# More unread identity matmuls in TensorE's waiting times: 31 places in place of 26, in a gated pair of state-space convolutions

## The chip, the cores and the metric

The kernel runs on one core of one Trainium2 chip. The metric is the device time of one execution in microseconds (us). Three runs of the kernel before gave 501.2, 500.29 and 502.1 us; their median is 501.2 us. The engines are called as the profile calls them: PE is TensorE (its matmuls; PEld is its weight loads), DVE is VectorE, ACT is ScalarE, POOL is GpSimd, and SP issues the DMA transfers.

## The reference

An input `x` of 2048 steps by 512 channels goes through two long convolutions, whose filters are sums over 128 complex exponentials in each channel, and a sigmoid of one weighted sum per step mixes the two results. All is float32. Cut to what matters:

```python
def reference(A_u, ..., gate_w):
    def _A_ref(u, A_re, A_im, B_re, B_im, C_re, C_im, log_dt, Dskip):
        dt = jnp.exp(log_dt)[:, None]
        P = jnp.exp((dt * (A_re + 1j * A_im))[:, :, None] * l[None, None, :])
        K = jnp.einsum("dn,dnl,dn->dl", Cc, P, dt * Bc).real
        return causal_convolution(u, K) + u * Dskip      # by FFT of length 2 L
    def _B_ref(u, log_A_real, A_imag, C_real, C_imag, log_dt, D_skip):
        P = jnp.exp((A * dt[:, None])[:, :, None] * pos[None, None, :])
        K = 2.0 * jnp.einsum("dn,dnl->dl", C, P).real
        return causal_convolution(u, K) + u * D_skip
    x = A_u
    g = sigmoid((x * gate_w).sum(-1, keepdims=True))
    return g * _A_ref(x, ...) + (1 - g) * _B_ref(x, ...)
```

(`causal_convolution` stands for the padded FFT, product and inverse FFT that the reference writes out.)

## The kernel before

The 512 channels are taken in four quarters, and each quarter has the two filters: eight filter stages (`NV = 8`). In each stage a filter is built in eight chunks (`chunk`). POOL writes phases `x` and magnitudes `E` (L584, L593, L604, L612), ACT takes sine and cosine of the phases into the PSUM tiles `sd` (L624 to L626), DVE multiplies them with the magnitudes into `QD` and `E` (L632 to L647), and PE sums the products (L663), 64 recorded matmuls a chunk. Every second chunk ACT copies the sums out (`K`, L686), and `put` (L707) takes them through a first Fourier step, two PSUM banks at a time, which ACT or DVE copies out to the tile `F` or `X` (L719). `forward` (L730) is the second Fourier step. For the input itself the same two steps run once for each quarter at the start (`stage1_u`, `stage2_u`; the copies after the second step are L765, written to DRAM at L772). For each filter stage the spectrum is multiplied by that of the input on DVE (`z`, L802 and L805), transformed back on PE (L814, L815), copied out by ACT (`st`, L818) and written to DRAM; `final` (L847) ends a quarter. The gate is a sum by matmul (L876) and a sigmoid.

The order of all this is set before any instruction is written. Each step is put on a list with its engine, a cost and a due time (`Plan.op`), and `Plan.run` plays the list through a model of the engines, the buffers and the PSUM banks, and takes in each engine the ready step with the earliest due time. The instructions are then written in the order found. An engine carries out its instructions in that order, and an instruction that writes into a PSUM bank waits until the last reader of that bank is done.

The table `FILL` (L81) adds matmuls whose result nobody reads. `turn` counts the steps of PE in the order found; where `turn` is a key of `FILL`, a call of `spare` (L143 on) stands in front of that step. It writes the given number of units, each a product of the 128x128 identity with itself, up to four units in one matmul (a matmul of four units is 128x512), into whichever free bank of `ps` or `sd` has been free longest in the model. The spare matmuls cost the model no time, so the table leaves the order of everything else as it is. In the profile they are the matmuls of L310.

A float32 matmul of this kernel appears in the profile as two weight loads and two matmuls: 4,839 matmuls of the program make the 9,678 of PE and 9,678 of PEld.

The lines in `run` that place a spare piece are these:

```python
if e == "T":
    if turn in FILL:
        order.append(self.spare(FILL[turn], min((f, t, i) for t in ("ps", "sd") for f, i in free[t])))
    turn += 1
```

Of the kernel before, what the change touches and what calls it, by code (L numbers as in the profile page):

```python
# [77 lines left out]
FW = -1.82  # L78


FILL = {18: 9, 37: 1, 41: 3, 67: 1, 90: 3, 145: 3, 150: 7, 154: 14, 191: 2, 197: 3, 199: 10, 220: 5, 269: 6, 304: 29, 33: 1, 36: 3, 40: 1, 61: 1, 104: 1, 149: 12, 189: 2, 196: 4, 198: 6, 248: 1, 249: 1, 5: 6}  # L81


def _flat(t):
# [27 lines left out]
class Plan:  # L112
# [44 lines left out]
    def run(self):  # L157
# [15 lines left out]
        while n < len(self.ops):  # L173
            nxt = 1e30
            for e in at:
# [32 lines left out]
# [4 lines that stand above are left out]
# [849 lines left out]
```

## Time and profile before

| | |
|---|---|
| median of three runs | 501.2 us |
| the profiled execution | 501.73 us, of which the span from the first to the last instruction is 499.9 us |
| mean granted clock of PE | 0.98 |
| busy: PE, DVE, ACT, POOL | 89%, 80%, 78%, 79% of the span |
| chain that ended last | PE 33%, ACT 27%, DVE 16%, POOL 11%, issue 10% |
| PE's spare matmuls (L310) | 94 recorded, from 21.1 us to 487.8 us |

The span is the time between the first and the last instruction; the execution's own time is 1.8 us more. Shares of busy time are averages over stages. The chain goes back from the last instruction, at each step to what released it, so that a line of the chain is a time that nothing else covered. "Idle before" names what ended the wait of an engine; "issue" there means that the engine waited for nothing that the profile shows. In the timeline and the chain the first number is the start and the second the duration, in us from the start of the span.

### The profile page before, as it was taken

How to read it: one execution, taken by the hardware profiler on the slowest of the kernel's cores; microseconds unless marked ns; L12 is line 12 of the kernel's file. 1: busy time of each engine (PE TensorE's matmuls, PEld its weight loads, DVE VectorE, ACT ScalarE, POOL GpSimd, SP SyncE). 2: the span in 40 equal slices, each digit the busy share in tenths (PEclk: the TensorE clock that was granted, in tenths of full speed). 3: DMA queues.
4: the chain of work that ended last, by engine and by line, in shares of the span. 5: the costliest groups of instructions: out<-in, count | busy, mean ns of one | idle time of the engine just before them, and what ended most of it. 6: DMA issues, size and time to landing. Idle time of an engine off the chain costs nothing.

```text
span 499.9 us, 22016 instructions
## 1 busy us (share of the span) xinstructions
PE 444.9 (89%) x9678; PEld 385.6 (77%) x9678; DVE 399.3 (80%) x569; ACT 387.6 (78%) x594; POOL 393.6 (79%) x365
## 2 busy tenths in 40 slices
PE   3669988989989999998998988999799999999996
PEld 3457876888567788875888877798689898898975
DVE  5759978998968998999978999879579989793420
ACT  5669969969898889789999889778698986771211
POOL 4586998955999999999799999769969999950000
PEclk9779999999999999998999999999899999999999
DMA  8938664685344365331327785263365144686835
GB/s 283 385 114 239 188 190 127 201 249 159 104 127 128 102 203 162 101 115 64 127 88 212 223 262 184 74 213 116 117 202 182 46 134 149 207 237 211 274 105 233
DMA packets 69439, 85.46 MB, mean 171 GB/s; under 512 B 4704, under 2 KB 50144, under 8 KB 69088
## 3 DMA queue, kind: packets, MB, share of 16 engines
q1 hardware_dynamic: 69344, 84.06, 53.1%
q8 instruction: 76, 1.25, 1.1%
q14 instruction: 19, 0.16, 0.1%
HBM read 50.49 MB, written 33.59 MB: 168 GB/s over the span
## 4 chain that ended last, share of the span: by engine, by line
PE 33%; ACT 27%; DVE 16%; POOL 11%; issue 10%; DMA 2%; DVEq 0%; SPq 0%; ACTq 0%; POOLq 0%
PE ps L730 7%; ACT sd L624 5%; PE ps L814 5%; PE ps L815 5%; PE ps L663 5%; PE ps L707 4%; PE ps L847 4%; DVE QD L632 4%; ACT x L625 3%; ACT sd L626 3%; POOL E L612 3%; DVE z L805 2%; DVE E L642 2%; ACT AB L522 2%; POOL x L584 2%
## 5 line engine op out<-in xcount | busy, mean ns | idle before, releaser
L612 POOL TENSOR_TENSOR E<-AB 128x1024 f32<-128x1024 f32 x64 | 125.2, 1957 | 0.1
L814 PE MATMUL ps<-z,c_t 128*128 128x128 f32 x512 | 103.1, 283 | 4.5 <-DVE z L802 2.8
L815 PE MATMUL ps<-z,c_t 128*128 128x128 f32 x512 | 100.2, 277 | 1.4 <-DVE z L805 0.7
L632 DVE TENSOR_TENSOR QD<-sd,E 128x1024 f32<-128x1024 f32 x64 | 77.8, 1216 | 19.6 <-ACT sd L624 8.9
L814 PEld LDWEIGHTS ps<-z,c_t 128*128 128x128 f32 x512 | 78.0, 192 | 11.0 <-DVE z L802 3.7
L730 PE MATMUL ps<-F,c_g 128*128 128x128 f32 x640 | 83.5, 278 | 1.4 <-DVE F L719 1.2
L624 ACT ACTIVATE sd<-x 128x1024 f32<-128x1024 int32 x64 | 66.0, 1030 | 21.0 <-POOL x L584 11.5
L815 PEld LDWEIGHTS ps<-z,c_t 128*128 128x128 f32 x512 | 77.8, 192 | 3.5 <-DVE z L805 3.5
L730 PEld LDWEIGHTS ps<-F,c_g 128*128 128x128 f32 x640 | 75.9, 188 | 4.4 <-ACT F L719 1.6
L642 DVE TENSOR_TENSOR E<-sd,E 128x1024 f32<-128x1024 f32 x64 | 77.5, 1212 | 1.0 <-ACT sd L626 1.0
L593 POOL TENSOR_TENSOR x<-pi,c_tm 128x512 int32<-128x512 int32 x64 | 68.3, 1067 | 12.6 <-ACT sd L626 8.8
L604 POOL TENSOR_TENSOR E<-AB 128x512 f32<-128x512 f32 x64 | 68.4, 1070 | 12.4 <-PE ps L663 8.6
L663 PE MATMUL ps<-E 128*32 128x64 f32 x2048 | 64.3, 223 | 5.7 <-DVE E L642 1.8
L626 ACT ACTIVATE sd<-x 128x1024 f32<-128x1024 f32 x64 | 66.0, 1031 | 3.8 <-PE sd L310 1.5
L625 ACT ACTIVATE x<-x 128x1024 f32<-128x1024 int32 x64 | 67.8, 1059 | 1.4
L584 POOL TENSOR_TENSOR x<-gh 128x512 int32<-128x512 int32 x64 | 68.4, 1069 | 0.2
L663 PE MATMUL ps<-QD 128*32 128x64 f32 x2048 | 63.7, 221 | 0.8 <-issue 0.8
L802 DVE TENSOR_TENSOR z<-ps,U 128x512 f32<-128x512 f32 x64 | 43.6, 682 | 24.9 <-PE ps L730 22.3
L818 ACT COPY st<-ps 128x512 f32<-128x512 f32 x64 | 37.2, 584 | 33.0 <-PE ps L815 27.6
L663 PEld LDWEIGHTS ps<-E 128*32 128x32 f32 x2048 | 47.7, 110 | 17.9 <-issue 8.1
L663 PEld LDWEIGHTS ps<-QD 128*32 128x32 f32 x2048 | 49.8, 111 | 1.1 <-issue 1.1
L707 PEld LDWEIGHTS ps<-w,K 64*64 64x64 f32 x2048 | 34.3, 134 | 18.9 <-issue 9.5
(123 smaller groups left out, 791.0 us busy)
## 6 DMA issues: line engine op xcount, KB each, us to landing
U<-ud SPq DMA_DIRECT2D x32, 512.0 KB, 3.9
wt<-st SPq DMA_DIRECT2D x64, 256.0 KB, 2.9
X<-wt SPq DMA_DIRECT2D x26, 512.0 KB, 5.6
ud<-z SPq DMA_DIRECT2D x32, 256.0 KB, 3.5
U<-in_u SPq DMA_DIRECT2D x16, 256.0 KB, 4.2
ud<-z SPq DMA_DIRECT2D x32, 128.0 KB, 3.6
U<-in_uT SPq DMA_DIRECT2D x16, 256.0 KB, 3.4
out<-st SPq DMA_DIRECT2D x16, 256.0 KB, 4.7
```

What stands on the lines that cost most here:

```text
L584: G.tensor_tensor(xi()[:, :, 1, :].rearrange("n c (a b) -> n c a b", a=4), t[:, :, 0:4].unsqueeze(3).to_broadcast([P, NCK, 4, 8]), t[:, :, ...
L604: G.tensor_tensor(Ev()[:, :, 0, :].rearrange("n c (a b) -> n c a b", a=4), A1()[:, ca, ::-1].unsqueeze(3).to_broadcast([P, NCK, 4, 8]), BB ...
L612: G.tensor_tensor(Ev()[:, :, 1:3, :].rearrange("n c w t -> n c (w t)"), AA()[:, ca].rearrange("n c w a -> n (c w) a").unsqueeze(3).to_broa ...
L624: op("A", 0.96, e, lambda: A.activation(bv(sn), wv(xi()), AF.Sin, scale=SCL), r=[x], w=[sn], func="S")
L625: op("A", 0.96, e, lambda: A.activation(x.t, x.v(dt=I32), AF.Abs), w=[x])
L626: op("A", 0.96, e, lambda: A.activation(bv(cs), wv(qv(x)), AF.Sin, bias=HALF_PI, scale=-SCL), r=[x], w=[cs], func="S")
L632: lambda: V.tensor_tensor(ev(QD)[:, :, 0::2, :], bv(sn).rearrange("n w c t -> n c w t"), Ev()[:, :, 0::2, :], ALU.mult),
L642: lambda: V.tensor_tensor(Ev()[:, :, 0:2, :], bv(cs)[:, 0].unsqueeze(2).to_broadcast([P, NCK, 2, NJ]), Ev()[:, :, 0:2, :], ALU.mult),
L663: T.matmul(K4[32 * b : 32 * b + 32, gg, :], ev(QD if w else E)[:, c, 2, :], ev(QD if w else E)[:, c, 0:2].rearrange("n h t -> n (h t)"), s ...
L730: T.matmul(b.v("p (k m h e) -> p m k h e", k=2, m=4, h=32, e=2)[:, mm], Gw[:, m, :], Fv(F)[:, :, m, :].rearrange("p (k h) e -> p k h e", k=2),
L814: T.matmul(o, Tw[:, m, 0:128], zv(Z1), start=True, stop=False)
L815: T.matmul(o, Tw[:, m, 64:192], zv(Z2), start=False, stop=True)
```

## The change

One line changes, the table of the spare units:

```diff
-FILL = {18: 9, 37: 1, 41: 3, 67: 1, 90: 3, 145: 3, 150: 7, 154: 14, 191: 2, 197: 3, 199: 10, 220: 5, 269: 6, 304: 29, 33: 1, 36: 3, 40: 1, 61: 1, 104: 1, 149: 12, 189: 2, 196: 4, 198: 6, 248: 1, 249: 1, 5: 6}
+FILL = {18: 9, 37: 1, 41: 3, 67: 2, 90: 3, 145: 3, 150: 7, 154: 14, 191: 2, 197: 3, 199: 10, 220: 5, 269: 6, 304: 29, 33: 1, 36: 3, 40: 1, 61: 1, 104: 1, 149: 15, 189: 2, 196: 5, 198: 6, 248: 1, 249: 1, 5: 6, 3: 11, 8: 16, 68: 2, 86: 2, 219: 8}
```

Five keys are new: 3 (11 units), 8 (16), 68 (2), 86 (2) and 219 (8). Three grow: 67 from 1 to 2, 149 from 12 to 15, 196 from 4 to 5. In all 44 units more, in 13 more matmuls, which are 52 more instructions of PE. DVE, ACT, POOL and SP have the same instructions in the same order as before.

On PE, between the second and the third `put` of the input (the first numbers are of banks: `ps_100` to `ps_103` are the four `ps` banks, `sd_104` and `sd_105` the two `sd` tiles; `w` is the matrix of the first step, `U` a piece of the input, `c_id` the identity):

```order
 L707 MATMUL ps_100<-w_117,U_83 64x64 x2
 L707 MATMUL ps_101<-w_117,U_83 64x64 x2
+L310 MATMUL sd_104<-c_id 128x512 x2
+L310 MATMUL sd_104<-c_id 128x384
 L707 MATMUL ps_102<-w_117,U_84 64x64 [waits DMAHW0_49,DVE_49]
 L707 MATMUL ps_102<-w_117,U_84 64x64
```

Eleven units now stand there, in an `sd` tile that nothing has used yet, and wait for nothing; the `put` behind them keeps its waits.

On PE, in front of the third and fourth `forward` of the input (`X` is the input after its first step, `c_g` the matrix of the second):

```order
 L707 MATMUL ps_101<-w_117,U_83 64x64 x2
 L707 MATMUL ps_103<-w_117,U_83 64x64 x2
-L730 MATMUL ps_102<-X,c_g 128x2x64 [waits DVE_49]
-L730 MATMUL ps_102<-X,c_g 128x2x64 x3
+L310 MATMUL ps_102<-c_id 128x512 [waits DVE_49]
+L310 MATMUL ps_102<-c_id 128x512 x3
+L730 MATMUL ps_102<-X,c_g 128x2x64 x4
 L730 MATMUL ps_100<-X,c_g 128x2x64 [waits DVE_49]
 L730 MATMUL ps_100<-X,c_g 128x2x64 x3
```

Sixteen units now stand in front of `forward`, in the same bank `ps_102` that `forward` writes; the wait for DVE, which empties that bank, has moved from `forward` to the first of the spare matmuls.

On PE, in front of the step of turn 219, a `put` of a filter (`z` are the products of the spectra, `K` the filter's sums):

```order
 L814 MATMUL ps_103<-z_79,c_t 128x128
 L815 MATMUL ps_103<-z_82,c_t 128x128
+L310 MATMUL ps_101<-c_id 128x512 [waits Activation_49]
+L310 MATMUL ps_101<-c_id 128x512
 L707 MATMUL ps_101<-w_117,K_78 64x64 [waits Activation_49]
 L707 MATMUL ps_101<-w_117,K_78 64x64
```

Eight units now stand between the last product of L815 and the `put`, in the bank that the `put` writes next.

## Prediction

> **What bounds the kernel now.** I read the page first: busy shares, granted clock, the code queue and the summary of the chain.
>
> ```profile
> PE 444.9 (89%) x9678; PEld 385.6 (77%) x9678; DVE 399.3 (80%) x569; ACT 387.6 (78%) x594; POOL 393.6 (79%) x365
> ...
> PEclk9779999999999999998999999999899999999999
> ...
> q8 instruction: 76, 1.25, 1.1%
> ...
> PE 33%; ACT 27%; DVE 16%; POOL 11%; issue 10%; DMA 2%; DVEq 0%; SPq 0%; ACTq 0%; POOLq 0%
> ```
>
> No engine is full, and the chain changes engine all the time. So a microsecond put on a link of the chain comes out at the end in full, while one taken away counts only until another engine is late. So the question at each new place of spare units is whether they run in one of PE's waits or behind it. The clock row has dips in slices 2, 3, 19 and 29. The chain shows what the one of slice 3 touches:
>
> ```profile
> 31.34 0.61 DVE z L765
> ...
> 31.99 3.78 PE ps L730 x16
> 35.77 1.48 PE ps L707 x64
> 37.26 1.10 PE ps L730 x8
> ```
>
> DVE empties a bank, PE starts `forward` 0.04 us later and works without a gap. The timeline of PE shows the idle stretches before these steps, and how the same step slows down after one:
>
> ```profile
> 16.37 1.99 PE L707 MATMUL ps<-w,U 64*64 64x64 f32 x64 [3.04 <-ACT X L719]
> 19.20 1.97 PE L707 MATMUL ps<-w,U 64*64 64x64 f32 x60 [0.85 <-DVE X L719]
> 21.11 2.46 PE L310 MATMUL sd<-c_id 128*128 128x512 f32 x4
> 24.19 2.02 PE L730 MATMUL ps<-X,c_g 128*128 128x128 f32 x16 [0.62 <-DMA c_g<-in_c_g]
> 26.14 1.16 PE L707 MATMUL ps<-w,U 64*64 64x64 f32 x64
> 31.99 3.78 PE L730 MATMUL ps<-X,c_g 128*128 128x128 f32 x16 [4.69 <-DVE z L765]
> 35.70 1.55 PE L707 MATMUL ps<-w,U 64*64 64x64 f32 x64
> ```
>
> Sixteen matmuls of L730 take 2.02 us at full clock and 3.78 after an idle 4.69; a `put` takes 1.16 or 1.97 to 1.99. The granted clock in stretches agrees (columns: stretch, length, busy time of PE, PEld, DVE, ACT, POOL, clock, DMA share, GB/s):
>
> ```profile
> 32.00:35.70 3.70, 3.70 (x16) 3.48 (x16) 3.02 (x5) 3.67 (x9) 3.70 (x3) 0.50 0.68 208
> 231.10:234.40 3.30, 3.30 (x5) 1.66 (x6) 2.99 (x5) 3.25 (x5) 3.30 (x9) 0.51 0.10 22
> 350.50:353.40 2.90, 0.05 (x4) 0.04 (x1) 2.39 (x4) 0.85 (x2) 2.82 (x5) 1.00 1.00 347
> 353.60:357.50 3.90, 3.90 (x70) 2.67 (x68) 0.63 (x2) 2.27 (x3) 3.33 (x3) 0.56 0.05 14
> ```
>
> Price of a unit:
>
> ```profile
> 225.48 2.74 PE L310 MATMUL ps<-c_id 128*128 128x512 f32 x6
> 231.10 3.31 PE L310 MATMUL ps<-c_id 128*128 128x512 f32 x4 [1.79 <-DVE F L719]
> ```
>
> The first is turn 149, 12 units in 2.74 us: 0.23 us each. The second is turn 150, 7 units at half clock: 0.47 us each.
>
> **The change part by part.**
>
> *Turn 8, 16 units.* This decides. The idle 4.69 us ends when DVE has emptied `ps_102`. The new units write that bank, so they carry the wait and start at 31.99, where `forward` started; nothing fills the idle time. They cost 16 x 0.228 = 3.65 us at full clock. They start at half clock, which lasted before until about 36.5 (the `put` of 35.70 took 1.55, about midway between 1.16 and 1.97). Until then some 9.5 units run, the other 6.5 take 1.5 us, end about 38.0; then L730 2.0 and L707 1.1, end about 41.1 against 37.25: +3.8. The slow stretch lasts as long either way and only meets other work, so the net is the full-clock length, and I take +3.65. Ends: +1.5 if PE were at full clock from the start (3.65 less 1.76 for L730 and 0.4 for L707), +7.5 if all 16 ran at 0.47. DVE queues behind: its next copy of L765 waits for this `forward`, and products on DVE, then ACT's sines, stand behind that copy, all of it in the chain.
>
> *Turn 3, 11 units.* These wait for nothing and take 11 x 0.228 = 2.5 us of the idle 3.04. They should hold the clock for the `put` of 16.37 (1.99 to 1.16, 0.8 us earlier). Behind that `put` DVE then meets ACT:
>
> ```profile
> 18.64 0.40 ACT L467 ACTIVATE fi<-AB 128x256 f32<-128x256 f32 x1
> 19.59 0.43 DVE L473 TENSOR_TENSOR ps<-p,fi 128x256 f32<-128x256 f32 x1
> 236.38 0.59 ACT L818 COPY st<-ps 128x512 f32<-128x512 f32 x1 [1.01 <-PE ps L815]
> ```
>
> L473 needs `fi`, ready at 19.04, so at most 0.5 of the 0.8 us gets through. I take -0.4, ends -2.5 (a shifted slow stretch takes the 1.76 and 0.4 at 31.99 too) and +0.5 (the units run partly at half clock).
>
> *Turn 219, 8 units.* Here PE waited for nothing shown, in the middle of a `put`:
>
> ```profile
> 349.43 1.08 PE ps L707 x61
> 350.51 2.85 issue
> 353.36 0.33 PE ps L707 x3
> 353.69 2.04 PE sd L310 x4
> 355.73 1.86 PE ps L663 x64
> ...
> 360.47 1.03 PE ps L663 x64
> ```
>
> The row of stretches has the DMA engines full (1.00, 347 GB/s) while PE stood still, and the code queue of the page brings 76 packets of 16.4 KB, one for 255 of PE's 19,356 loads and matmuls. I read the 2.85 us as a late piece of code. If it comes at the same time, 8 units (1.83 us) in front are free, 1.0 us of waiting is left, and the clock need not fall to 0.56: the 5 units of turn 220 take 1.15 in place of 2.04, L663 1.03 in place of 1.86, together 1.7, of which 0.2 goes again, since more of the `put` is left behind the cut (below). I take -1.5; ends -2.8 (the code also comes 1 us earlier) and +1.8 (the wait stays as long, behind the units).
>
> *Turn 149, 3 more units,* 0.7 us in the idle 1.79 before 231.10: hidden. With less idle time the 7 units of 231.10 may take 1.6 in place of 3.31, but ACT, next in the chain, waited only 1.01 at 236.38. I take -0.5, ends -1.0 and +0.7.
>
> *Turns 67, 68, 86, 196:* 1, 2, 2 and 1 units, 0.23 to 0.46 us each, each ahead of a wait that is longer:
>
> ```profile
> 113.63 0.49 PE L814 MATMUL ps<-z,c_t 128*128 128x128 f32 x2 [1.11 <-DVE z L802]
> 138.76 0.32 PE L663 MATMUL ps<-E 128*32 128x64 f32 x8 [1.46 <-POOL E L604]
> 309.68 1.15 PE L707 MATMUL ps<-w,K 64*64 64x64 f32 x60 [0.28 <-ACT st L858]
> ```
>
> Turns 67 and 68 share the 1.11 (0.7 needed), 86 has the 1.46 (0.46), 196 the 0.28 (0.23). I take 0; without cover they cost 1.4 together.
>
> *52 more instructions.* The pieces of code are cut by count, so every cut falls 28 instructions earlier in the program after turn 8, and 52 after turn 219. Waits of this kind in PE:
>
> ```profile
> PE ps L707 <- issue: 6.7, 6, 2.9
> PE ps L663 <- issue: 2.6, 5, 1.1
> PE ps L847 <- issue: 0.6, 1, 0.6
> ...
> 72.63 0.34 PE L707 MATMUL ps<-w,K 64*64 64x64 f32 x8 [0.86 <-issue]
> ...
> 81.69 0.58 PE L707 MATMUL ps<-w,K 64*64 64x64 f32 x25 [0.87 <-issue]
> ...
> 421.43 0.34 PE L707 MATMUL ps<-w,K 64*64 64x64 f32 x7 [0.85 <-issue]
> ```
>
> Twelve waits, 9.9 us, nearly all in runs of the short matmuls L707 and L663, where 256 instructions last only some 2.1 us. A run of 64 records has 128 instructions; a cut with 8, 25 or 7 records left has enough of the run ahead of it that 28 to 52 instructions less leave it inside. So most old waits stay, while some of the 60-odd free cuts move from long matmuls (14 records of L730 are 1.7 us) into short runs. More waits are likelier than fewer. I take +2.0, an estimate: two or three new waits of the 0.85 us size. Ends: -3 (a third of the 9.9 goes) and +8 (nearly as many again). The Trainium skill (Runtime: NRT & Kernel Launch, Instruction fetch mechanics) says that code comes in 16 KiB blocks of 256 instructions and that crossing a block's edge is mostly hidden. The size agrees with the row, the hiding not at these twelve waits; by it this term would be 0 and the sum 1.25 us.
>
> Sum: +3.65 - 0.4 - 1.5 - 0.5 + 0 + 2.0 = +3.25. The profiled execution took 501.73 us (span 499.9 and 1.8 around it), so its like would be 505.0. It stands 0.5 above the median of 501.2; on that I forecast 504.5.
>
> **The rivals.**
>
> *The cuts cost no more than now.* Then +1.25, 502.5 us. For it: the present waits depend on DMA traffic as much as on the cut. Against: twelve waits now, and only a small part of the cuts has one.
>
> *The cuts fall badly.* The last term is +5 to +8 in place of +2: 507.5 to 510.5 us. For it: the waits are 0.2 to 2.9 us each, and six new ones are enough.
>
> *The cuts fall well.* This one ends faster. Place: the twelve waits. Price: up to the 9.9 us. If the term is under -2.75, the sum is under -1.5; at -4 it is 498.5 us. For it: the 2.85 us at 350.51 is one wait alone, and it may go whole. Against: the runs are longer than the shift.
>
> *The new units don't do what they are for,* at turn 3 and 219 as well: the clock falls anyway. Then 3.65 + 0 + 0 + 0 + 2 = 5.65, 506.9 us. The Trainium skill (TensorE: Matmul & The Clock Gate, Part 1, What's actually happening) says that the window by which activity is judged runs freely, so that slow stretches differ from run to run, and advises against fitting to one count of them. One trace here can't show that; by it the gains of turns 3, 149 and 219 are the uncertain ones and the cost of turn 8 is not.
>
> **How the numbers follow.** Forecast 0.42, cuts as now 0.21, cuts badly 0.16, clock falls anyway 0.12, cuts well 0.09. A change under 0.3% (1.5 us, 499.7 to 502.7) is about what runs of this kernel can't tell from none; the three runs spread by 1.8 us. The forecast's own range is 503 to 506. Slower by more than that: the forecast, the two worse cases and a third of "as now" (its centre lies at the bound), 0.77. Same: the rest of "as now" and a little of the forecast, 0.14. Faster: 0.09. The range goes from 500.4 (turns 219 and 149 at their better ends, cuts at -0.25: 3.65 - 0.4 - 2.8 - 1.0 - 0.25 = -0.8) to 509.5 (cuts at +7, the rest as taken: 1.25 + 7).
>
> **What would show it.** Right: L310 starts at about 31.6 to 32.0 right behind DVE's copy, with PE idle before it from 27.3 as now, and lasts 5 to 6 us; `forward` behind it takes 2.0; the chain has L310 there. L310 at 13.3 lasts 2.5 and the next `put` 1.2. In front of 349.4 L310 lasts 1.8, the "issue" wait in that `put` is 1 us or less, L663 behind it 1.03. The "issue" waits of PE add up to 11 to 13 us. Wrong: L310 of turn 8 ends before DVE's copy does (it then lies in the idle time, and -2.2 takes the place of +3.65), or the "issue" waits differ by more than 5 us.

## The result, and the profile after

| | median | lowest to highest | runs |
|---|---|---|---|
| before | 501.34 us | 500.29 to 502.1 | 4 |
| changed | 508.32 us | 505.37 to 514.17 | 4 |

The ratio is 1.0121, with a 95% interval of 1.0073 to 1.017. The changed kernel is slower by 1.2%. The ratios here and below leave out single runs more than 1.5% above the fastest of their kernel, here that of 514.17 us, so they need not be the quotient of the two medians. It was run again beside the experiments: 509.45 us against 499.74 us, ratio 1.0169 (1.0124 to 1.0214). The first execution profiled was the longest of all its runs (514.17 us), so the profile shown here is one of the second series, of 509.79 us (span 507.9), close to its median.

The page of the changed kernel, the rows that answer to those of before (busy time by engine; granted clock by slice; the queue of DMA that brings the instructions, called the code queue here; the chain by engine):

```profile
PE 453.6 (89%) x9704; PEld 387.4 (76%) x9704; DVE 399.1 (79%) x569; ACT 387.9 (76%) x594; POOL 393.8 (78%) x365
...
PEclk9979899999999999999999999999999999999999
...
q8 instruction: 76, 1.25, 1.1%
...
PE 41%; ACT 22%; DVE 16%; issue 9%; DMA 5%; POOL 5%; SPq 0%; DVEq 0%; ACTq 0%; POOLq 0%
```

PE is busy 8.7 us longer and has 41% of the chain in place of 33%. Of the dips of the clock, those of slices 2, 19 and 29 are gone, that of slice 3 is still there, and a new one stands in slice 5. In the execution of 514.17 us the dips stand in slices 3, 9, 16 and 37, so most of them belong to an execution and not to the kernel. Where the time went shows in the starts of the same instructions. DVE, ACT and POOL have the same instructions in the same order in both kernels, so each start can be taken from its fellow in the profile of before. The table gives the median of these delays around some places (us of the profile of before; a minus is earlier), for the changed kernel and for five kernels of the experiments:

| place | 18 | 30 | 45 | 55 | 105 | 165 | 215 | 350 | 375 | 425 | 455 | 490 |
|---|---|---|---|---|---|---|---|---|---|---|---|---|
| changed | +0.1 | +1.1 | +5.0 | +7.1 | +7.0 | +7.0 | +8.2 | +7.9 | +5.1 | +6.0 | +8.1 | +8.1 |
| cuts_only | -0.1 | -0.1 | -0.5 | +2.0 | +3.0 | +3.0 | +4.8 | +5.1 | +2.1 | +2.4 | +6.8 | +7.0 |
| t8_alone | 0.0 | 0.0 | +3.0 | +2.9 | +1.5 | +1.9 | +2.0 | +3.3 | -0.1 | +0.6 | +0.6 | +0.7 |
| t219_alone | +0.2 | +0.2 | +0.9 | +0.8 | +0.9 | +0.9 | +1.4 | +1.4 | -1.7 | +0.9 | +0.9 | +1.1 |
| t5_units | -0.1 | -0.1 | -1.1 | -0.9 | -1.1 | -1.1 | -1.1 | -1.1 | -0.9 | 0.0 | +0.2 | +0.3 |
| t8_to_t5 | -0.2 | -0.4 | -1.0 | -1.0 | -2.2 | -1.8 | -1.6 | -0.9 | -3.1 | -2.6 | +1.0 | +1.3 |

These are single executions, that of the kernel before too, and some lie off the median of their runs: that of cuts_only 2.9 us over it, that of t8_alone 2.9 us under it, that of t219_alone 2.0 us over it. They show where time goes; how much an edit costs is told by the ratios.

The largest step of the changed kernel lies between 30 and 45. Its chain of waits there:

```profile
32.47 0.61 DVE z L765
33.08 0.04 issue
33.12 6.19 PE ps L310 x8
39.31 1.78 PE ps L730 x16
41.09 1.09 PE ps L707 x64
...
48.27 0.26 PE ps L707 x4
48.54 1.84 issue
```

L310 starts 0.04 us behind DVE's copy, where `forward` started before, and all of it is in the chain. The timeline of PE has the rest of the first 60 us:

```profile
13.79 4.55 PE L310 MATMUL sd<-c_id 128*128 128x512 f32 x6
18.26 1.26 PE L707 MATMUL ps<-w,U 64*64 64x64 f32 x68
...
33.12 6.19 PE L310 MATMUL ps<-c_id 128*128 128x512 f32 x8 [5.46 <-DVE z L765]
39.15 1.95 PE L730 MATMUL ps<-X,c_g 128*128 128x128 f32 x16
41.02 1.16 PE L707 MATMUL ps<-w,U 64*64 64x64 f32 x64
...
50.38 1.15 PE L707 MATMUL ps<-w,U 64*64 64x64 f32 x60 [1.84 <-issue]
51.46 3.90 PE L310 MATMUL ps<-c_id 128*128 128x512 f32 x6
```

At turn 3 the 11 units took 4.55 us in place of 2.5, longer than the idle time they stand in, and the `put` behind them started at 18.26 in place of 16.37. At turn 8 PE stood idle for 5.46 us and then worked 6.19 us on the units. The `put` that has a cut waited 1.84 us for code in place of 0.97, and the spare units after it, which are in both kernels, took 3.90 in place of 2.21: the clock had fallen. The granted clock of these two stretches is the third number from the end, 0.59 and 0.55:

```profile
33.12:39.31 6.19, 6.19 (x10) 2.73 (x11) 1.74 (x3) 6.16 (x17) 4.67 (x4) 0.59 0.42 128
51.46:54.93 3.47, 3.47 (x8) 1.52 (x6) 3.47 (x5) 2.79 (x4) 3.37 (x3) 0.55 0.71 220
```

### The profile page after: what moved, and what is told of

Read it like the earlier page. It is cut to its first block, busy times and chain, and to the rows that moved or that the text cites. A ratio compares the mean times of both kernels' runs of the same rounds, so it can differ in the third digit from the quotient of the medians.

```text
span 512.3 us, 22068 instructions
## 1 busy us (share of the span) xinstructions
PE 458.0 (89%) x9704; PEld 393.1 (77%) x9704; DVE 399.3 (78%) x569; ACT 388.0 (76%) x594; POOL 393.9 (77%) x365
## 3 DMA queue, kind: packets, MB, share of 16 engines
q8 instruction: 76, 1.25, 1.1%
## 4 chain that ended last, share of the span: by engine, by line
PE 44%; ACT 23%; DVE 15%; issue 9%; DMA 4%; POOL 4%; DVEq 0%; SPq 0%; ACTq 0%; POOLq 0%
PE ps L730 9%; PE ps L814 6%; PE ps L815 6%; PE ps L663 6%; PE ps L707 6%; ACT sd L624 5%; PE ps L847 4%; PE ps L310 4%; ACT x L625 3%; DVE QD L632 3%; DVE z L805 2%; ACT sd L626 2%; ACT st L818 2%; DVE E L642 1%; ACT AB L522 1%
## 5 line engine op out<-in xcount | busy, mean ns | idle before, releaser
L814 PE MATMUL ps<-z,c_t 128*128 128x128 f32 x512 | 103.8, 285 | 6.2 <-issue 2.3
L815 PE MATMUL ps<-z,c_t 128*128 128x128 f32 x512 | 101.2, 279 | 2.2 <-issue 0.9
L814 PEld LDWEIGHTS ps<-z,c_t 128*128 128x128 f32 x512 | 78.8, 194 | 13.0 <-issue 4.7
L730 PE MATMUL ps<-F,c_g 128*128 128x128 f32 x640 | 85.0, 281 | 3.8 <-DVE E L647 2.2
L730 PEld LDWEIGHTS ps<-F,c_g 128*128 128x128 f32 x640 | 77.3, 192 | 6.9 <-DVE E L647 2.3
L815 PEld LDWEIGHTS ps<-z,c_t 128*128 128x128 f32 x512 | 78.7, 194 | 3.8 <-DVE z L805 3.2
L663 PE MATMUL ps<-E 128*32 128x64 f32 x2048 | 63.8, 222 | 2.5 <-DVE E L642 1.7
L663 PE MATMUL ps<-QD 128*32 128x64 f32 x2048 | 62.5, 219 | 1.5 <-issue 1.5
L663 PEld LDWEIGHTS ps<-E 128*32 128x32 f32 x2048 | 47.6, 109 | 14.0 <-issue 4.4
L663 PEld LDWEIGHTS ps<-QD 128*32 128x32 f32 x2048 | 49.3, 110 | 1.8 <-issue 1.8
L805 DVE SCALAR_TENSOR_TENSOR z<-ps,sgn,U 128x512 f32<-128x512 f32 x64 | 47.4, 740 | 0.1
```

Source lines behind the costliest of these rows:

```text
L663: T.matmul(K4[32 * b : 32 * b + 32, gg, :], ev(QD if w else E)[:, c, 2, :], ev(QD if w else E)[:, c, 0:2].rearrange("n h t -> n (h t)"), s ...
L730: T.matmul(b.v("p (k m h e) -> p m k h e", k=2, m=4, h=32, e=2)[:, mm], Gw[:, m, :], Fv(F)[:, :, m, :].rearrange("p (k h) e -> p k h e", k=2),
L814: T.matmul(o, Tw[:, m, 0:128], zv(Z1), start=True, stop=False)
L815: T.matmul(o, Tw[:, m, 64:192], zv(Z2), start=False, stop=True)
```

## Experiments

All leave the rest of the program and its order as they are; what they add are matmuls that nobody reads. A "small matmul" multiplies a 32-column slice of the identity with 64 of its columns; like every matmul here it is four instructions, and eight records of it took 0.44 us. `before` in the table is the median of runs of the kernel before in the same series; "shift" is how many instructions earlier the cuts of PE's code fall in the last tenth of the program (256 is one whole piece, so cuts fall where they fell).

| kernel | shift | median | before | ratio and 95% interval |
|---|---|---|---|---|
| after_again | 52 | 509.45 | 499.74 | 1.0169 (1.0124 to 1.0214) |
| cuts_only | 52 | 505.84 | 499.74 | 1.0099 (1.0068 to 1.013) |
| t8_alone | 16 | 505.36 | 499.74 | 1.009 (1.0054 to 1.0127) |
| no_t8 | 36 | 501.92 | 499.74 | 1.0034 (1.0003 to 1.0064) |
| pad64 | 256 | 503.02 | 500.55 | 1.0054 (1.0025 to 1.0082) |
| t8_pad | 256 | 506.36 | 500.55 | 1.0135 (1.0088 to 1.0182) |
| t8_sd | 16 | 507.66 | 500.55 | 1.0158 (1.01 to 1.0215) |
| t219_alone | 8 | 500.93 | 500.55 | 1.0013 (0.998 to 1.0047) |
| t5_units | 24 | 501.92 | 501.92 | 0.9985 (0.9943 to 1.0028) |
| t5_pad | 256 | 504.29 | 501.92 | 1.0051 (1.0011 to 1.0091) |
| pad3 | 256 | 504.18 | 501.92 | 1.0048 (1.0007 to 1.0089) |
| t8_to_t5 | 52 | 504.28 | 501.19 | 1.0067 (1.0032 to 1.0102) |

**The change again.**

> The changed kernel as it is, for more runs of it and a profile of one that is not the slowest. Both theories: the median lies at 506 to 509 us, 5 to 8 us over the kernel before. Theory 'behind the wait' (the 16 units of turn 8 cost their 3.65 us on the path, the rest comes from code that is cut elsewhere): DVE's copy behind the third forward starts 3 to 4 us later than before in any profile, and the rest of the delay sits at waits of PE called issue.

Measured: ratio 1.0169, median 509.45 us, a little over the 506 to 509 of both theories. This is the second series of the result, and the profile shown above is of it.

**The cuts without the units** (cuts_only): the table of before, and at each place where the change adds matmuls as many small ones.

```diff
+TINY = {3: 3, 8: 4, 68: 1, 86: 1, 149: 1, 196: 1, 219: 2}
+                    if turn in TINY:
+                        order.append(self.spare(0, min(...), TINY[turn]))
```

> No new spare units; at each of the seven places where the change adds matmuls stand as many small matmuls (32 columns of weights, 64 moving columns, 13 in all, 52 instructions, some 0.4 us together). Only the places at which PE's code is cut move. Theory 'the cuts cost': 2 to 6 us slower than before. Rival 'the units themselves cost all': within 1 us of before.

Measured: ratio 1.0099, that is 5 us (3.4 to 6.5). The small matmuls themselves are little: the four of turn 8 took 0.44 us, the two of turn 219 0.31. So 52 instructions, by moving the cuts, cost more than the 16 units were thought to cost. One place shows how. `L673` is the last step before a run of products (`L814`, `L815`) near the end. In the kernel before, then the changed kernel, the run without turn 8 (no_t8) and the two with a shift of 52 (t8_to_t5, cuts_only; lines are six further in the last):

```profile
451.24 0.39 PE L673 MATMUL ps<-dskip,c_id 128*128 128x8 f32 x2
451.49 0.47 PE L814 MATMUL ps<-z,c_t 128*128 128x128 f32 x2
```

```profile
457.44 0.39 PE L673 MATMUL ps<-dskip,c_id 128*128 128x8 f32 x2
459.91 0.46 PE L814 MATMUL ps<-z,c_t 128*128 128x128 f32 x2 [2.08 <-issue]
```

```profile
451.40 0.39 PE L673 MATMUL ps<-dskip,c_id 128*128 128x8 f32 x2
...
453.77 0.27 PE L815 MATMUL ps<-z,c_t 128*128 128x128 f32 x1 [1.10 <-issue]
```

```profile
450.14 0.39 PE L673 MATMUL ps<-dskip,c_id 128*128 128x8 f32 x2
452.88 0.46 PE L814 MATMUL ps<-z,c_t 128*128 128x128 f32 x2 [2.35 <-issue]
```

```profile
454.59 0.39 PE L679 MATMUL ps<-dskip,c_id 128*128 128x8 f32 x2
457.04 0.46 PE L820 MATMUL ps<-z,c_t 128*128 128x128 f32 x2 [2.06 <-issue]
...
458.47 0.64 PE L820 MATMUL ps<-z,c_t 128*128 128x128 f32 x2
```

PE goes on 2.4 to 2.7 us after the start of L673 in each of the four, wherever the cut is. With a shift of 36 seven records of the products still lie ahead of the cut and cover 1.0 us of that; with 52 the cut stands in front of the first of them, and all is a wait. With a shift of 24 (t5_units) it is 0.41 us, at 8 (t219_alone) none, at 16 none in t8_alone and 0.37 in t8_sd; in the kernel before the cut lies still further on, and there is none. The DMA records agree: the transfer of the next 16,384 bytes of code starts 0.0 to 0.5 us after the start of L673 in the six kernels that wait. So the code comes at about the same moment after L673, and the wait grows with each instruction by which the cut moves ahead of that moment. And a wait is not always the whole price: in cuts_only the matmuls from 458.47 on take 0.64 for 0.39, since the clock fell behind the wait (granted clock 0.50 from 458.5 to 461.6); the delay grows by 3.5 us there (from +3.3 at 450 to +6.8 at 455), against a wait of 2.06. In the changed kernel the clock stayed up behind the same wait, and the delay grew by 1.9 (6.2 to 8.1).

**Turn 8 alone** (t8_alone: the table of before with `8: 16`), **and all but turn 8** (no_t8: the table of the change without it).

> Of the change only turn 8: 16 units behind DVE's wait, 16 more instructions. Theory 'behind the wait': +3.65 us from the units, and 0 to 3 from the cuts that fall 16 instructions earlier, so 3.5 to 6.5 us slower. Rival 'the units warm the array and pay for themselves': within 1.5 us of before.

> The change without turn 8: 28 units of the 44, 36 more instructions. Theory 'behind the wait': 3.65 us less than the whole change, so 1 to 4 us slower than before, because the gains of turns 3, 149 and 219 (2.4 us together) are outweighed by the cuts. Rival 'turn 8 is harmless': like the whole change, 5 to 8 us slower than before.

Measured: 1.009 and 1.0034. Turn 8 alone is 4.5 us (2.7 to 6.3), with whatever its 16 instructions do to the cuts; all the rest together is 1.7 (0.1 to 3.2). Against the changed kernel of the same series (1.0169) leaving turn 8 out is worth some 6.7 us. The rest holds no gain: three places that were meant to keep the clock up, and the cuts of 36 instructions, end above zero. In the profile of t8_alone the units are L310 at 31.96, 5.40 us, behind a wait of 4.38 for DVE.

**Is it the wait for DVE, or the place?** (t8_sd: the same 16 units at the same turn, but into the second `sd` tile, which DVE's copy has nothing to do with.) The spare products are written there, and in pad64 and t8_pad too, over the cosines of one chunk, which ACT has just put down and DVE reads later; that chunk is then formed from other numbers, with the same instructions.

```diff
+AT = {8: ('sd', 1)}
-    order.append(self.spare(FILL[turn], min(...)))
+    order.append(self.spare(FILL[turn], (0.0, *AT[turn]) if turn in AT else min(...)))
```

> Turn 8's 16 units with the same 16 instructions, but into the sd tile that nothing uses until 31.2 us, so that they need not wait for DVE's copy. They should run from 27.3 to 31.0 and the third forward take 2.0 us in place of 3.78. Theory 'behind the wait': 3.65 + 2.1 = 5 to 6 us faster than turn 8 alone as the change has it, so 1.5 us faster to 0.5 us slower than before. Rival 'the cuts are all': as turn 8 alone.

Measured: 1.0158, not better than t8_alone (the intervals overlap). The timeline of PE in t8_sd, where L311 is the spare matmul:

```profile
32.27 5.65 PE L311 MATMUL sd<-c_id 128*128 128x512 f32 x8 [5.11 <-ACT sd L627]
37.76 1.95 PE L731 MATMUL ps<-X,c_g 128*128 128x128 f32 x16
```

The units waited as long, for another engine: ACT was writing cosines into that tile until 32.2. It starts on them only at 31.2, but in the order of the program they stand ahead of turn 8, so units placed there come behind them. The expectation overlooked this, and so the run does not try the units inside the idle time. In the order as it is, all four banks hold results at turn 8 that DVE copies out only from 31.2 on, and the `sd` tiles are taken by sines and cosines. So another of these tiles in place of `ps_102` does not help at turn 8.

**Cuts held in place** (pad64: 64 small matmuls at turn 8, 256 instructions; t8_pad: 60 of them, and the 16 units).

```diff
+PAD = {8: (64, 'sd', 1)}
+                    if turn in PAD:
+                        order.append(self.spare(0, (0.0, *PAD[turn][1:]), PAD[turn][0]))
```

> No new spare units; 64 small matmuls (256 instructions, as many as one piece of code holds) at turn 8, into the sd tile that is free until ACT's cosine at 31.2, so they run in the idle 4.7 us before the third forward. Behind them all cuts fall where they fell before. Theory 'the cuts cost by where they fall': within 1.5 us of before, 3 us or more under the run of small matmuls that moved the cuts by up to 52. Rival 'more instructions cost, wherever the cuts fall': 4 us or more slower than before.

> Turn 8's 16 units behind DVE's wait, as in the change, with 60 small matmuls in the idle time ahead of them: 256 instructions together, so the cuts behind fall where they fell before. Theory 'behind the wait': 3 to 4.5 us over the run with 64 small matmuls alone. Rival 'turn 8 costs only by its cuts': as that run.

Measured: 1.0054 and 1.0135. They did not come out as a clean test. The filling itself, written into the same `sd` tile, stands behind ACT's cosines (3.64 us at 32.11 in pad64), and the `put` at the next cut, with 18 records ahead of it as before, waited 2.08 us in both where it waited 0.97. Units and filling together are 7.1 us of PE at that place (3.40 and 3.70), of which 2.2 come back since `forward` (1.95) and `put` (1.16) then run at full clock, and 1.1 come on top by the longer wait: 6.0, against 6.8 measured (4.4 to 9.1). By the medians t8_pad lies 3.3 us over pad64, inside the 3 to 4.5 of the theory. That the cost of turn 8 stays when cuts are held agrees with units on the path; how much moved cuts add to turn 8 alone these two don't tell.

**Turn 219 alone** (the table of before with `219: 8`).

> Of the change only turn 219: 8 units in front of the put whose code comes late. 8 more instructions, behind 350 us. Theory of the prediction: 1.5 us faster than before (2.8 at best). Rival 'the wait only moves behind the units': 0.5 to 2 us slower.

Measured: 1.0013 (0.998 to 1.0047): nothing. In its profile the wait of 2.85 us is gone and the table of delays drops by 3.1 there, more than forecast; then the next `put` with a cut waits, the clock falls behind that (the matmuls of L847 take 0.64 for 0.39), and 2.6 are given back:

```profile
420.77 0.69 PE L707 MATMUL ps<-w,K 64*64 64x64 f32 x11 [2.05 <-issue]
421.39 0.69 PE L847 MATMUL ps<-X 128*64 128x128 f32 x4
421.87 0.64 PE L847 MATMUL ps<-X,wg 128*64 128x128 f32 x4
```

Nor are the units what brings the 3: t8_alone and cuts_only have no unit there and drop by 3.4 and 3.0 (waits of 1.21 and 1.30), and t5_units, with its cuts 24 instructions earlier, waits there for 3.10:

```profile
352.41 0.46 PE L707 MATMUL ps<-w,K 64*64 64x64 f32 x15 [3.10 <-issue]
```

**The units in front of the wait** (t5_units: `5: 30` in place of 6). The spare matmuls of turn 5 stand two steps earlier, at 21 us, in an `sd` tile that is free then. More of them there push the `forward` and the `put` behind them into the idle time, where nothing waits for them.

> Theory (units that stand behind the wait for a bank cost their length; the same work in front of it, in PE's idle time, costs nothing and keeps the clock up): the 24 units run from about 21 to 27, forward and put behind them end by 31.2, PE's wait for DVE at 32 is 1 us or less in place of 4.7, L730 of 32 takes 2.0 in place of 3.78 and the put behind it 1.2, so the program is about 2 us earlier at 38; the cuts of PE's code fall 24 instructions earlier and give back 0 to 3: 498 to 501 us where the kernel before has 500. Rival (what costs is more spare work and moved cuts, wherever it stands): 503 to 506, as with 16 units at turn 8 (505.4).

Measured: 0.9985 (0.9943 to 1.0028). With 24 units more than before no difference from before is shown; 16 at turn 8 cost 0.9% in their series. The timeline of PE:

```profile
21.04 7.33 PE L310 MATMUL sd<-c_id 128*128 128x512 f32 x16
28.21 1.95 PE L730 MATMUL ps<-X,c_g 128*128 128x128 f32 x16
...
31.92 2.05 PE L730 MATMUL ps<-X,c_g 128*128 128x128 f32 x16 [0.67 <-DVE z L765]
33.91 1.16 PE L707 MATMUL ps<-w,U 64*64 64x64 f32 x64
...
43.75 1.09 PE L707 MATMUL ps<-w,U 64*64 64x64 f32 x58 [2.00 <-issue]
```

```profile
32.00:35.70 3.70, 3.70 (x86) 3.51 (x87) 3.70 (x7) 3.67 (x9) 3.70 (x3) 1.00 0.63 193
```

The idle 4.69 us are 0.67, the clock is 1.00 in the stretch where it was 0.50, `forward` takes 2.05 for 3.78, and PE is 2.2 us earlier at 35.00 than at 37.19. That is what units in the idle time were to do. It does not arrive: the next `put` waits 2.00 us for code in place of 0.97, and goes on at 43.75 where it went on at 44.80, so 1.1 us are left, and those are gone after 400 (the table of delays).

**The same with cuts held in place** (t5_pad: `5: 22` and 60 small matmuls at turn 5), **and the filling alone, in idle time** (pad3: 64 small matmuls at turn 3).

> Sixteen more units at turn 5 and 60 small matmuls (64 columns, of a 32-column slice of the identity), 256 instructions together, so that every cut behind them falls where it fell before. Theory: the same 2 us at 38, and nothing of it given back by moved cuts: 497.5 to 499.5. Rival (extra instructions cost whatever the cuts): 502 or more, as the 64 small matmuls at turn 8 (503.0).

> Only 64 small matmuls at turn 3, 256 instructions in PE's idle 3.0 us, so one piece of code more and every cut behind it as before. Theory (a cut's place costs, and units on the path; not the number of instructions): within 1 us of the kernel before. Rival (each further piece of code costs): 1 to 3 us slower, as the same 64 matmuls at turn 8, which took 3.6 us there, 2.5 us net.

Measured: 1.0051 and 1.0048, 2.5 and 2.4 us, both against the theory. The timeline of PE in pad3:

```profile
13.44 2.29 PE L316 MATMUL sd<-c_id 128*32 128x64 f32 x90
17.73 0.76 PE L316 MATMUL sd<-c_id 128*32 128x64 f32 x38 [2.00 <-issue]
18.42 2.15 PE L713 MATMUL ps<-w,U 64*64 64x64 f32 x68
21.27 0.91 PE L713 MATMUL ps<-w,U 64*64 64x64 f32 x21 [0.70 <-DVE X L725]
23.92 1.34 PE L713 MATMUL ps<-w,U 64*64 64x64 f32 x39 [1.74 <-issue]
```

A piece of small matmuls lasts so short a time that PE waits for the next piece inside it (2.00 us) and again one piece later (1.74); the `put` starts at 18.42, 2 us late. In t5_pad such a wait is 1.36 us, and the `put` ends at 35.3, where the idle time was over at 32. So a whole piece of filling does not restore the program of before: it brings its own waits for code, and neither run tells what cuts cost by their place alone.

**The change with its 16 units moved** (t8_to_t5): the same 52 instructions, and every cut behind turn 8 where the change has it.

```diff
-FILL = {..., 5: 6, 3: 11, 8: 16, 68: 2, 86: 2, 219: 8}
+FILL = {..., 5: 22, 3: 11, 68: 2, 86: 2, 219: 8}
```

> The whole change, with the 16 units of turn 8 in front of turn 6 (turn 5 has 22 in place of 6): the same 52 instructions more and, behind turn 8, every cut where the change has it. Theory (units behind the wait for DVE cost their length, in the idle time before it nothing): the program is 1 to 2 us earlier than the kernel before at 38 to 42 where the changed kernel was 1.4 later at 40 and 5 later at 45; behind that the cuts of the change cost what they cost there, so that it ends 5 to 7 us under the changed kernel: 501 to 504 us, ratio 1.000 to 1.008 to the kernel before. Rival (the place of the cuts makes nearly all of the loss, as in the run with small matmuls alone, 1.010): 505 to 508, ratio 1.010 to 1.017.

Measured: 1.0067 (1.0032 to 1.0102), inside what the theory said, at its worse end, and some 3 to 5 us under the changed kernel (1.0121 and 1.0169). These are other series, each against the kernel before; the interval of the first overlaps with this one, that of the second does not. The profile has it 3.1 us ahead of before at 375, and 1.0 behind at 455: the waits of 1.30 at 441.70 and of 2.35 at 452.88 (shown above), both at cuts that the 52 instructions moved. The clock at 32 was not held here (L730 took 3.48), since PE came to turn 5 earlier and the units had ended by 24.9, so the 2.2 us of t5_units were not to be had; 0.4 was, at 30, by turn 3.

No kernel of these is shown to beat the one before.

## Why the prediction was right, and where it was not

The direction was right, and 508.3 lies inside the range of 500.4 to 509.5. It does not lie where the likeliest case put it (503 to 506) but in the rival of badly fallen cuts (507.5 to 510.5), which had 0.16. The second series, 509.45, lies at the very edge of the range. The range held in part by luck: the cuts cost more than was taken, and the gain at turn 219 came without the cause that was given for it. Step by step:

*Turn 8, +3.65.* Right in place, kind and size. PE idle from 27.7 to 33.1, L310 right behind the copy, 6.2 us long where 5 to 6 was written (it started 1.1 later by turn 3, and at half clock; in the execution of 514.17 us it started at 32.01 and took 5.67), `forward` 1.95 and `put` 1.16 behind it. PE ends the `put` 4.9 later than before (42.18 against 37.26), 3.8 without the 1.1. Removing the units from that place is worth 0.5 to 1.0% (the changed kernel against t8_to_t5, from different series), and t8_alone, with a small shift of the cuts in it, is 4.5 us.

*Turn 3, -0.4, worst +0.5.* Mis-sized: +1.1 in the profile of the changed kernel, -0.3 in that of t8_to_t5. The step that failed is "2.5 us of the idle 3.04": it took full clock for granted. The units ran 4.55 us in this execution of the changed kernel, 3.52 in its other one, 3.31 in t8_to_t5 and 4.24 in no_t8, so in the first the `put` started 1.9 us late, and DVE's copy behind it moved from 18.46 to 19.59. The Trainium skill (TensorE: Matmul & The Clock Gate, Part 1, What's actually happening) says that the clock is low until PE has been busy for a window and that windows run freely; four lengths of the same 11 units in four executions agree.

*Turn 219, -1.5.* The stretch gave -2.8 in the changed kernel, the better end: L310 1.72, the wait 0.09, L663 1.03, as written:

```profile
357.20 1.72 PE ps L310 x4
358.92 0.72 PE ps L707 x35
359.64 0.09 issue
359.73 0.69 PE ps L707 x29
360.42 1.28 PE sd L310 x4
361.69 1.03 PE ps L663 x64
```

But the cause was not what the step said. Kernels without these units have the same drop, and the units alone are worth nothing in the end. The wait is late code, as the prediction read it: by the DMA records PE goes on 1.3 to 1.5 us after the code has landed in the kernel before, t5_units, t8_alone and cuts_only. Its length goes with the start of that transfer: 0.5 us after PE has stopped in the kernel before (2.85) and 0.6 after in t5_units (3.10), but 1.1 ahead in t8_alone (1.21) and 0.9 ahead in cuts_only (1.30). What sets that start is open, and whether 2.85 is the usual wait of the kernel before, of which there is one profile, is not known.

*Turn 149, -0.5.* The 7 units of turn 150 took 1.77 for 3.31, as written (1.6), and the delay went from 8.2 at 215 to 8.0 at 260: -0.2. Turns 67, 68, 86 and 196 cost nothing: the delay is 7.0 both at 105 and at 165, and 7.9 to 8.0 from 280 to 350.

*52 more instructions, +2.0.* This is the term that was mis-sized most. With small matmuls in place of the units it measured +5.0 (3.4 to 6.5). The reason given, free cuts that move into places where code is late, holds; the price does not. It counted two or three waits at 0.85 us each. The new waits are larger, 2.1 to 2.35 at one place alone, and behind some of them the clock falls, so that the work there takes up to twice its time (the spare units at 51.46 in the changed kernel, +1.7). Nor were all of the twelve old waits at cuts: 0.21 us at 342.57 and 0.58 at 371.06 do not stand a whole number of 256 instructions from the others, so ten waits, 9.1 us, were late code. That the sum of the waits shown as "issue" came out as forecast (12.0, 11 to 13 written; 9.9 before) was no confirmation: one old wait shrank from 2.85 to 0.09 meanwhile, and the price of a wait is not its length. By the Trainium skill (Runtime: NRT & Kernel Launch, Instruction fetch mechanics) crossing a block is mostly hidden. In number that holds: the profiles of these kernels show 9 to 19 waits each, nearly all at cuts, of some 75 pieces. In time it does not, with 7.5 to 16 us of waits in one execution.

*The sum.* 1.25 without cuts, 3.25 with them. With turn 8 kept at 3.65, which the profile bears out, and what the runs show for the rest, -0.4 to +1.1 (turn 3), -0.2 (turn 149) and 5.0 (the cuts, turn 219's stretch included, since cuts_only has that drop too), it is 8.0 to 9.6. By the ratios the two series measured 6.1 (3.7 to 8.5) and 8.4 (6.2 to 10.7). The sum lies inside the second of these ranges, and only its lower end inside the first; terms from single executions and from runs with intervals of 3 us do not add up closer.

*Within 0.3% can't be told from none; the three runs spread by 1.8.* Too narrow. Over 29 runs on one chip the kernel before goes from 496.94 to 506.53. A dozen runs and more of each kernel still leave 0.3 to 0.4% to each side of a ratio.

## What to carry to other kernels

Work meant to fill an engine's idle time must be placed ahead of the wait that makes the engine idle, and needs a buffer that is free during that wait; behind it the same work is paid in full (0.9% for 16 units behind, moved cuts included; none shown for 24 ahead). An insertion into a long program moves every cut of its code behind it: measure that by itself, with the same number of instructions and next to no work, before the insertion is judged by what it does in place. A gain in one stage of an engine that is fed late with code may only turn into a longer wait at the next cut, as in t5_units and t219_alone.

## What the runs showed of the hardware

- The long waits called "issue" are late code. In the kernel before ten of the twelve stand a whole number of 256 PE instructions apart (give or take one), and PE goes on 1.2 to 1.6 us after a transfer of 16,384 bytes on the code queue has landed.
- The wait at a cut depends on more than its place. The `put` at 44.8 has its cut behind 18 records in six kernels, and waited 0.61, 0.97, 1.07, 1.24, 2.08 and 2.08 us.
- Near the end PE went on 2.4 to 2.9 us after L673's start in the six kernels that wait there (453.55 against 451.19 in t5_units, 455.88 against 452.98 in t8_sd), whatever the shift of the cut. Counted from the cut before it, which lies in a run of short matmuls and hardly moves in time, it is 4.1 to 4.6 us, as even; which of the two sets it is not shown.
- Short matmuls use up code faster than it comes: 128 records of small matmuls (256 instructions) took 3.05 us in pad3, and PE waited 2.00 us inside them.
- Two executions of the changed kernel wait for different times at the same cuts: 1.84 and 0.79 us at 50.38 and 111.27 in one, 2.13 and 2.33 at 49.04 and 110.63 in the other.
